# Attention prologue, conversions, projection tile and row-sum constant of a fused attention and feed-forward kernel

## The chip, the cores and the metric

The kernel runs on one core of a Trainium2 chip. The core has TensorE (PE) for matmuls, VectorE (DVE), ScalarE (ACT), GpSimd (POOL) and SyncE (SP), which here only issues DMAs; each engine works through its own queue in order, and semaphores order the queues against each other. The metric is the device time in microseconds, median of several runs; smaller is better. [...]

## The reference

Three stages follow each other. Attention works on 2 batches x 8 heads of 768 tokens with 64 columns. Six random projections give each query and key a bucket of six sign bits, and a query sees only keys of its bucket:

```python
q_bits = (np.einsum('bhsd,dk->bhsk', q, proj) > 0)      # likewise k_bits
mask = q_bucket[:, :, :, None] == k_bucket[:, :, None, :]
scores = np.where(mask, scale * q @ k.T, -1e9)
attn = np.exp(scores - scores.max(-1))
attn = attn / (attn.sum(-1) + 1e-09);  out = attn @ v
```

Then comes a feed-forward with a rational activation, on 1536 tokens: `h = x @ w_in` (512 to 2048), `g = P(h) / (Q(h) + 1e-6)`, `g @ w_out`. Last is a mixture of eight experts with ReLU, whose weights per token come from eight rounds of row and column scaling of a softmax. `w_in` and `w_out` arrive as 64-bit floats; everything else is 32-bit.

## The kernel before, in words

Matmul operands are split into a rounded upper half and a remainder, the lower half (`split`, L95), so that a product is three fast matmuls instead of a slow one.

**Heads.** `load_head` (L119) loads q, k and v of a head into one of two buffers. `prep_head_a` (L225) splits them (head 0's q and k on VectorE, all else on GpSimd), transposes q and k on TensorE against the identity `idr`, and lets ScalarE copy the result into `a1` and `b1`, of which two DMAs make the lower rows of `a2` and `b2`. `prep_head_b` (L251) multiplies by the projections in two column pieces, 512 and 256, each in a single bank (`hp`); VectorE compares each piece with thresholds `thr` into `bits`, and two DMAs put these rows into `a2` and `b2`. Scores multiply `a1` by `b1` and `a2` by `b2` into the same sum, so that unequal buckets push a score down.

**Groups.** A head has three groups of two query tiles, 48 groups in all, one for each iteration of the loop at L720. `scores` (L270) makes four matmuls for each of the two tiles into one of two double banks (`s`); VectorE copies the tile and accumulates its minimum (the scores are negated), and ScalarE takes the exponential with the row sum as its accumulator. `norm` (L288) has VectorE add 1e-9 by a reduce over pairs (sum, 1e-9), take the reciprocal, and GpSimd scale the two tiles. Two iterations later `trans` (L298) transposes the scaled tiles on TensorE in three pieces, each through one of four single banks (`pt`), to an upper half (ScalarE, `pth`) and a lower half (VectorE, `ptl`). One iteration after that `values` (L314) multiplies by v. Head preparations stand in the first two iterations of the head before.

**Weights.** A 64-bit tile of 128 columns is loaded raw (`load_weights`, two buffers per matrix) and converted (`prep_weights`, L188): ScalarE's absolute value and GpSimd's clamp (`narrow_a`), four integer and float operations on VectorE (`narrow_b`, L173), GpSimd's addition (`narrow_c`), ScalarE's upper half, GpSimd's lower half. Eight conversions (four tiles of each matrix) are written into attention at iterations 35, 38, 41 and 44 (`wprep`, L718); there their scratch `c` lies in SBUF. Those of later quarters run in the feed-forward, with scratch in PSUM.

**Order.** In the prologue and in attention the order on each engine is not the written one: a planner sorts the instructions by its own model of their times and may pull one far forward. So the first two conversions (L180 to L183) run before the first scores, and the constants of the feed-forward (L722 to L738) stand in VectorE's queue in the middle of the prologue. From the feed-forward on (L806) the written order is kept on TensorE, ScalarE, VectorE and GpSimd. Its first part has 48 steps; each makes a hidden tile (`gemm1`, one of three banks `h`), its activation (`activate_a`, L366: ScalarE, GpSimd's product `tq`, VectorE's five operations), and from step 6 on also the second product (`gemm2_a`).

## Time and profile before

| | us |
|---|---|
| runs: median (lowest to highest) | 1589.35 (1587.63 to 1591.01) |
| profiled execution, its time | 1589.4 |
| its span | 1587.6 |
| TensorE busy | 1536.8 (97%) |
| VectorE busy | 1199.3 (76%) |
| GpSimd busy | 938.9 (59%) |
| ScalarE busy | 622.1 (39%) |
| in attention, mean of one: minimum (768 columns, VectorE) | 0.949 |
| lower half of transposed weights (512 columns, VectorE) | 0.682 |
| scaling (768 columns, GpSimd) | 0.937 |
| split of q (384 columns, GpSimd): upper half, lower half | 0.531, 1.013 |

Busy time is the time in which an engine had an instruction in work; for TensorE this includes matmuls whose neighbours wait. A share over the whole span mixes three stages with different limits: attention (to about 291 us), the first feed-forward (to about 640 us) and the experts, where TensorE is busy without a gap. What the first two stages wait for is read from their own stretches.

### The profile page before, as it was taken

The numbers are of one execution on the slowest core, as the hardware profiler recorded it, in microseconds if no ns is written. First come the engines' busy times: TensorE is split into PE (matmuls) and PEld (weight loads), VectorE is DVE, ScalarE is ACT, GpSimd is POOL, SyncE is SP. The second block draws the span as 40 slices with busy tenths as digits, with TensorE's granted clock in tenths as the row PEclk, the third lists the DMA queues.
The fourth block names the chain that finished last, engine by engine and source line by source line (L and its number), as shares of the span: only waits on it lengthen the run. The fifth ranks groups of instructions, "written<-read, shape, count | busy, mean of one in ns | idle before, by whom it ended". The sixth has DMA issues, their size and how long they took to land.

```text
span 1587.6 us, 22241 instructions
## 1 busy us (share of the span) xinstructions
PE 1536.8 (97%) x8071; PEld 1355.8 (85%) x8071; DVE 1199.3 (76%) x2116; ACT 622.1 (39%) x1167; POOL 938.9 (59%) x1165
## 2 busy tenths in 40 slices
PE   5989999899999999999999999999999999999999
PEld 4888889687777877889899999989899998989898
DVE  7989999799999984886666766676666666666665
ACT  4878888788777842111111111111111111111111
POOL 6777875577777976456644653564465356436530
PEclk8999999999999999999999999999999999999999
DMA  5322221021212000101010110101011001101002
GB/s 170 86 83 79 81 70 25 14 67 54 66 53 67 14 27 27 41 27 40 27 41 27 41 40 27 36 32 40 27 40 41 27 28 40 40 27 40 14 1 80
DMA packets 49406, 71.85 MB, mean 45 GB/s; under 512 B 4368, under 2 KB 35088, under 8 KB 49296
## 3 DMA queue, kind: packets, MB, share of 16 engines
q1 hardware_dynamic: 48432, 68.85, 14.1%
q8 instruction: 64, 1.05, 0.3%
q10 hardware_dynamic: 864, 1.57, 0.3%
q14 instruction: 46, 0.38, 0.1%
HBM read 59.79 MB, written 3.15 MB: 40 GB/s over the span
## 4 chain that ended last, share of the span: by engine, by line
PE 65%; DVE 2%; ACT 0%; issue 0%; DVEq 0%; ACTq 0%
PE accb L599 33%; PE prod L534 29%; PE acca L405 2%; PE h L354 1%; PE lp L635 0%; DVE t L470 0%; DVE t L473 0%; DVE c L559 0%; DVE part L417 0%; DVE gl L555 0%; ACT xb L106 0%; DVE t L480 0%; ACT gh L554 0%; DVE t L484 0%; DVE csum L676 0%
## 5 line engine op out<-in xcount | busy, mean ns | idle before, releaser
L534 PE MATMUL prod<-xb,ww 128*128 128x384 f32 x2688 | 481.7, 336 | 1.8 <-ACT m L106 1.3
L599 PE MATMUL accb<-wb,gh 128*128 128x512 f32 x1536 | 475.7, 391 | 2.9 <-ACT osum L106 2.5
L534 PEld LDWEIGHTS prod<-xb,ww 128*128 128x128 f32 x2688 | 469.8, 188 | 8.0 <-ACT m L106 1.6
L610 DVE SCALAR_TENSOR_TENSOR osum<-accb,gp,osum 128x512 f32<-128x512 f32 x336 | 251.7, 749 | 127.7 <-PE accb L599 126.0
L599 PEld LDWEIGHTS accb<-wb,gh 128*128 128x128 f32 x1536 | 287.0, 188 | 60.9 <-ACT osum L106 2.9
L599 PE MATMUL accb<-wb,gl 128*128 128x512 f32 x768 | 300.9, 392 | 0.4 <-DVE gl L555 0.4
L100 POOL TENSOR_SCALAR wb<-rb 128x512 fp32r<-128x512 f32 x64 | 40.2, 627 | 405.8 <-PE accb L599 405.8
L554 ACT ACTIVATE gh<-c 128x384 fp32r<-128x384 f32 x256 | 134.3, 526 | 352.5 <-DVE c L559 352.1
L106 ACT ACTIVATE m<-prod 128x384 f32<-128x384 f32 x64 | 31.5, 492 | 457.9 <-PE prod L534 457.9
L599 PEld LDWEIGHTS accb<-wb,gl 128*128 128x128 f32 x768 | 144.2, 188 | 32.0 <-DVE gl L555 1.7
L555 DVE SCALAR_TENSOR_TENSOR gl<-c,gh 128x384 fp32r<-128x384 f32 x256 | 165.2, 645 | 1.3 <-ACT gh L554 0.9
L559 DVE TENSOR_TENSOR c<-prod,u 128x384 f32<-128x384 f32 x192 | 106.6, 558 | 61.7 <-PE prod L534 54.1
L354 PE MATMUL h<-xh,wa 128*128 128x512 f32 x384 | 126.7, 392 | 3.4 <-DVE tu L377 3.4
L405 PE MATMUL acca<-gh,wb 128*128 128x512 f32 x384 | 126.4, 391 | 2.8 <-DVE part L417 1.7
L109 DVE TENSOR_TENSOR ptl<-pt,pth 128x512 fp32r<-128x512 f32 x144 | 94.5, 682 | 19.1 <-ACT pth L106 18.3
L559 DVE TENSOR_TENSOR c<-prod,m 128x384 f32<-128x384 f32 x64 | 35.7, 558 | 92.4 <-PE prod L534 92.4
L103 POOL TENSOR_TENSOR ww<-ra,ww 128x256 fp32r<-128x256 f32 x128 | 95.4, 746 | 10.7
L294 POOL TENSOR_SCALAR e<-e,rs 128x768 f32<-128x768 f32 x96 | 88.8, 937 | 20.8 <-DVE rs L292 11.3
L308 PE MATMUL pt<-idr,e 128*128 128x128 f32 x576 | 83.0, 279 | 11.1 <-DVE ptl L109 4.9
L285 DVE TENSOR_SCALAR_CACHE_REDUCE e<-s 128x768 f32<-128x768 f32 x96 | 90.9, 949 | 2.1 <-PE s L278 1.7
L286 ACT ACTIVATE e<-e,nm 128x768 f32<-128x768 f32 x96 | 89.9, 936 | 3.8 <-DVE e L285 3.1
L354 PEld LDWEIGHTS h<-xh,wa 128*128 128x128 f32 x384 | 72.1, 188 | 22.4 <-DVE tu L377 5.9
(168 smaller groups left out, 2546.3 us busy)
## 6 DMA issues: line engine op xcount, KB each, us to landing
ra<-in_moe_w_dram SPq DMA_DIRECT2D x32, 512.0 KB
rb<-in_moe_w_dram SPq DMA_DIRECT2D x32, 512.0 KB
ra<-in_moe_w_in_dram SPq DMA_DIRECT2D x16, 512.0 KB
rb<-in_moe_w_out_dram SPq DMA_DIRECT2D x16, 512.0 KB
qkv<-in_q_dram SPq DMA_DIRECT2D x16, 192.0 KB
qkv<-in_k_dram SPq DMA_DIRECT2D x16, 192.0 KB
qkv<-in_v_dram SPq DMA_DIRECT2D x16, 192.0 KB
a<-a SPq DMA_DIRECT2D x16, 192.0 KB
```

Source lines behind the costliest of these rows:

```text
L103: pool.tensor_tensor(lo, src, hi.bitcast(F32), ALU.subtract)
L109: dve.tensor_tensor(lo, src, hi.bitcast(F32), ALU.subtract)
L285: dve.tensor_scalar(e[j], s[:, 0:S], BIG, None, ALU.min, ALU.min, accum_out=nm)
L286: act.activation(e[j], e[j], AF.Exp, bias=nm, scale=-1.0, accum_out=rs[:, j, 0:1])
L354: pe.matmul(hps, lhsT=a[:, c], rhs=x[:, c], start=m == 0, stop=m == 3 * KC - 1)
L405: pe.matmul(o, lhsT=l[:, js], rhs=r, start=f == 0 and m == 0, stop=f == QF - 1 and m == 2)
L534: pe.matmul(o, lhsT=w[:, i, c], rhs=x[:, j, c], start=n == 0, stop=n == 5)
L554: act.activation(gh, c, AF.Relu)
L555: low.append(lambda: dve.scalar_tensor_tensor(gl, c, 0.0, gh.bitcast(F32), ALU.max, ALU.subtract))
L559: dve.tensor_tensor(c, o, x, ALU.add)
L599: pe.matmul(o, lhsT=l[:, ts], rhs=r, start=n == 0 and m == 0, stop=n == 1 and m == 2)
L610: dve.scalar_tensor_tensor(d, o, gate["p"][:, n, e:e + 1], d, ALU.mult, ALU.add)
```

## The change

- **Prologue.** proj is loaded between k and v of head 0. The identity is rounded by ScalarE instead of VectorE. The thresholds are made ahead of head 0's preparation. Head 0's compared bits are sent by SyncE and ScalarE, one DMA each. Head 2's load, the raw weights' loads and the constants' loads are ordered behind these sends; the constants move from iteration 2 to 10.
- **Projections.** The two column pieces go into one double bank, taken from the two that the scores use, and are compared by one instruction of 768 columns.
- **Row sums.** The row sums have a tile of their own, and GpSimd adds 1e-9; the reciprocal stays on VectorE.
- **Conversions.** In attention run six of the eight, cut into pieces: two chains of three, a piece of each at set iterations from 4 to 41, ordered behind that iteration's minimum on VectorE, exponential on ScalarE and scaling on GpSimd. Their VectorE scratch lies in PSUM (a single bank). Two conversions, of `w_out`'s tiles 2 and 3, move to the start of the feed-forward.

`tc.issue_after(x)` orders what its block makes behind instruction x in the queue of x's engine; it adds no semaphore.

```diff
-    def narrow_b(bits, c):
-        ci = c.bitcast(I32)
-        pc = sum_bank(3, "bits") if bits_in_psum else c
-        pi = pc.bitcast(I32)
+    def narrow_b1(bits, c, pi):
+        dve.tensor_scalar(pi, c.bitcast(I32), 5, 2, ALU.logical_shift_left, ALU.logical_shift_right)
+        high = bits[:, :, 1]
+        dve.scalar_tensor_tensor(high, high, -0x40000000, pi, ALU.bitwise_and, ALU.bitwise_or)
+
+    def narrow_b2(bits, pi):
...
-            narrow_b(bits, n)
+            if in_attention:
+                narrow_b1(bits, n, bank("bits").bitcast(I32))
+                yield
+                narrow_b2(bits, bank("bits").bitcast(I32))
+            else:
+                pi = sum_bank(3, "bits").bitcast(I32)
+                narrow_b1(bits, n, pi)
+                narrow_b2(bits, pi)
...
+        hp = two_banks("hp").rearrange("p a n -> p (a n)")
         for n0, n1 in COLS:
-            hp = bank("hp")[0:KROW + 2 * NB, 0:n1 - n0]
...
-            dve.tensor_scalar(bits[QROW:KROW + 2 * NB, n0:n1], hp[QROW:], ...)
+        compared = dve.tensor_scalar(bits[rows], hp[rows, 0:S], thr[rows, 0:1], thr[rows, 1:2], ALU.is_ge, ALU.mult)
+        sent = sp.dma_start(a2[QROW:QROW + 2 * NB].bitcast(F32), ...)
+        sent_k = (sp if i else act).dma_start(b2[QROW:QROW + 2 * NB].bitcast(F32), ...)
...
-        dve.tensor_reduce(rs, rs_eps, AX.X, ALU.add)
+        pool.tensor_scalar(rs, rsum, 1e-9, None, ALU.add)
         dve.reciprocal(rs, rs)
...
-    wprep = {NG - 13 + 3 * j: j for j in range(QF)}
+    converting = [convert((0, 0), (0, 1), (0, 3)), convert((1, 0), (1, 1), (0, 2))]
+    CSTEPS = 3 * 5 + 1
+    csteps = {}
+    for m in range(2):
+        for n in range(CSTEPS):
+            csteps.setdefault(4 + m + n * (NG - 9) // CSTEPS, []).append(m)
...
+        for m in csteps.get(it, ()):
+            with behind(minimum, exped, scaled):
+                next(converting[m], None)
...
-    narrowing, acting, summing = [], [], []
+    narrowing, acting, summing = [prep_weights(1, i) for i in (2, 3)], [], []
...
+        for w in narrowing + narrowing:
+            go(w)
         for s in range(NS + QF):
```

## Rows read from the trace of the kernel before

**Rows 1.** The page, part 1: busy us, share of span, instructions.

```profile
PE 1536.8 (97%) x8071; PEld 1355.8 (85%) x8071; DVE 1199.3 (76%) x2116; ACT 622.1 (39%) x1167; POOL 938.9 (59%) x1165
```

**Rows 2.** Stretches: length, busy PE, PEld, DVE, ACT, POOL, clock, DMA share, GB/s.

```profile
0.00:24.20 24.20, 9.49 (x48) 7.13 (x48) 17.31 (x48) 6.43 (x12) 16.03 (x25) 0.95 0.62 178
24.20:291.10 266.90, 252.08 (x1813) 228.00 (x1814) 241.09 (x533) 215.27 (x453) 196.19 (x241) 0.97 0.26 72
```

**Rows 3.** Timeline, prologue: start, duration, engine, line, instruction [idle before and releaser].

```profile
4.54 0.56 DVE L109 TENSOR_TENSOR sk<-qkv,sk 128x384 fp32r<-128x384 f32 x1
...
6.42 0.43 DVE L699 CAST pjr<-pjz 128x512 fp32r<-128x512 f32 x1
...
9.40 0.21 DVE L135 CAST idr<-eye 128x128 fp32r<-128x128 f32 x1
...
9.67 1.00 PE L245 MATMUL tp<-idr,sq 128*128 128x128 f32 x6 [9.67 <-DVE rowf L705]
...
13.61 1.21 DVE L180 TENSOR_SCALAR c<-c 128x512 int32<-128x512 int32 x1 [2.29 <-POOL c L170]
...
13.86 0.63 PE L259 MATMUL hp<-b,pjr 128*108 128x256 f32 x2
...
18.13 0.76 SPq L263 DMA_DIRECT2D b<-bits  x1
...
20.53 0.47 PE L278 MATMUL s<-b,a 76*128 76x512 f32 x1 [1.42 <-DMA b<-bits]
...
24.20 0.96 DVE L285 TENSOR_SCALAR_CACHE_REDUCE e<-s 128x768 f32<-128x768 f32 x1
```

**Rows 4.** Stretch of attention, instructions on tile c alone: DVE, ACT, POOL busy.

```profile
24.20:291.10 266.90, 22.17 (x24) 8.47 (x13) 20.13 (x21) 0.97 0.26 72
```

**Rows 5.** Line 180 by forms: duration ns least/median/most, first and last start.

```profile
L180 DVE TENSOR_SCALAR bits<-c x24: 685/689/690, 308.9 to 507.8; 128x512 int32<-128x512 int32 x24
L180 DVE TENSOR_SCALAR c<-c x8: 405/893/1220, 13.6 to 177.7; 128x512 int32<-128x512 int32 x8
```

**Rows 6.** VectorE, 24.2 to 291.1: waits (total, times, longest), then groups.

```profile
DVE ptl L109 <- ACT pth L106: 18.3, 17, 2.4
...
L260 DVE TENSOR_SCALAR bits<-hp,thr 44x512 fp32r<-44x512 f32 x14 | 11.5, 820 | 0.5
L260 DVE TENSOR_SCALAR bits<-hp,thr 44x256 fp32r<-44x256 f32 x15 | 8.3, 556 | 0.1
```

**Rows 7.** Timeline, VectorE: a reduce of row sums and what follows.

```profile
269.32 0.15 DVE L291 TENSOR_REDUCE rs<-rse 128x2 f32<-128x4 f32 x1
269.41 0.96 DVE L285 TENSOR_SCALAR_CACHE_REDUCE e<-s 128x768 f32<-128x768 f32 x1
```

**Rows 8.** Timeline, TensorE without waits: projections, then values, scores, transposes.

```profile
257.94 0.63 PE L259 MATMUL hp<-a,pjr 128*108 128x512 f32 x2
...
259.33 0.40 PE L277 MATMUL s<-b,a 128*128 128x512 f32 x1
...
264.04 0.96 PE L323 MATMUL av<-pth,sv 128*128 128x256 f32 x6
...
265.56 0.40 PE L277 MATMUL s<-b,a 128*128 128x512 f32 x1
...
266.27 1.04 PE L308 MATMUL pt<-idr,e 128*128 128x128 f32 x8
267.06 0.48 PE L277 MATMUL s<-b,a 128*128 128x512 f32 x1
```

**Rows 9.** GpSimd, 24.2 to 291.1: a wait, and a group.

```profile
POOL e L294 <- DVE rs L292: 11.3, 11, 2.5
...
L100 POOL TENSOR_SCALAR xh<-xp 128x256 fp32r<-128x256 f32 x23 | 9.5, 413 | 12.1 <-DVE xp L334 12.1
```

**Rows 10.** Timeline, start of the feed-forward.

```profile
294.52 1.29 POOL L375 TENSOR_TENSOR tq<-tq,tw 128x512 f32<-128x512 f32 x1 [2.15 <-ACT tq L373]
...
295.14 0.69 DVE L376 TENSOR_TENSOR tu<-tu,h 128x512 f32<-128x512 f32 x1 [4.08 <-ACT tu L374]
...
304.93 0.50 PE L354 MATMUL h<-xh,wa 128*128 128x512 f32 x1 [1.06 <-DVE tu L377]
...
311.96 1.04 POOL L186 TENSOR_TENSOR c<-ra 128x512 f32<-128x512 f32 x1 [1.95 <-DVE ra L183]
```

More of the change, by code (lines that the diff above doesn't have):

```diff
@@ L6 @@
-from contextlib import ExitStack
+from contextlib import ExitStack, contextmanager, nullcontext
 from itertools import count
@@ L72 @@
     FP = F2 // P // 2
-    WLOAD = 3
-    CONST_AT = 2
+    WLOAD = 2
+    CONST_AT = 10
     EB = 6
@@ L117, with load_head @@
     loaded = {}
-    def load_head(i):
+    def load_head(i, between=None):
         b, h = heads[i]
@@ L122, in load_head, with load_proj @@
         for j, src in enumerate((q, k, v)):
+            if j == 2 and between:
+                between()
             sp.dma_start(t[:, j], src[b, h].rearrange("(p c) d -> p c d", c=C))
         loaded[i] = t
-    load_head(0)
     pj = ap.tile([P, NB], F32, tag="pj", bufs=1, name="pj")
-    sp.dma_start(pj[0:D, :], proj)
-    sp.dma_start(pj[D:2 * D, :], proj)
+    def load_proj():
+        sp.dma_start(pj[0:D, :], proj)
+        sp.dma_start(pj[D:2 * D, :], proj)
+    load_head(0, load_proj)
     load_head(1)
@@ L233, in prep_head_a @@
             hi, lo = (dve.tensor_copy, dve_lo) if i == 0 and j < 2 else (pool_hi, pool_lo)
-            split(hi, lo, d[:, :, h0:h0 + D], d[:, :, l0:l0 + D], t[:, j])
-        if i + 2 < len(heads):
+            with tc.issue_after(last) if i == 1 and j == 2 else nullcontext():
+                made = split(hi, lo, d[:, :, h0:h0 + D], d[:, :, l0:l0 + D], t[:, j])
+            if j == 1:
+                splitted, last = made, made.ins
+        if 0 < i < len(heads) - 2:
             load_head(i + 2)
@@ L683, with behind @@
     NG = len(heads) * G
-    prep_head_a(0)
-    pjz = ap.tile([P, 4, P], F32, tag="e", bufs=EB, name="pjz")
-    dve.memset(pjz, 0.0)
-    pjh = ap.tile([P, NB], F32R, tag="pjh", bufs=1, name="pjh")
-    dve.tensor_copy(pjh, pj)
-    pjl = ap.tile([P, NB], F32, tag="pjl", bufs=1, name="pjl")
-    dve.tensor_tensor(pjl, pj, pjh.bitcast(F32), ALU.subtract)
-    for j, row, half in ((0, QROW, slice(0, P)), (1, QROW, slice(0, D)), (2, KROW, slice(0, P)), (3, KROW, slice(D, P))):
-        src = pjh.bitcast(F32) if j % 2 == 0 else pjl
-        dve.tensor_scalar(pjz[half, j, row:row + NB], src[half], -1.0, None, ALU.mult)
-        dve.tensor_copy(pjz[half, j, row + NB:row + 2 * NB], src[half])
-    pjr = ap.tile([P, 4, P], F32R, tag="pjr", bufs=1, name="pjr")
-    dve.tensor_copy(pjr, pjz)
+    @contextmanager
+    def behind(*made):
+        with ExitStack() as stack:
+            for m in made:
+                stack.enter_context(tc.issue_after(m.ins))
+            yield
     row = ap.tile([P, 1], I32, tag="row", bufs=1, name="row")
@@ L713 @@
     dve.tensor_scalar(rowf[:, 2:3], rowf[:, 0:1], -1.0, F_BELOW, ALU.add, ALU.mult)
-    dve.tensor_tensor(thr[:, 0:1], thr[:, 0:1], rowf[:, 2:3], ALU.add)
-    prep_head_b(0)
-    wprep = {NG - 13 + 3 * j: j for j in range(QF)}
-    bits_in_psum = False
+    thr_made = dve.tensor_tensor(thr[:, 0:1], thr[:, 0:1], rowf[:, 2:3], ALU.add)
+    with behind(thr_made):
+        first_split, _ = prep_head_a(0)
+    pjz = ap.tile([P, 4, P], F32, tag="e", bufs=EB, name="pjz")
+    dve.memset(pjz, 0.0)
+    pjh = ap.tile([P, NB], F32R, tag="pjh", bufs=1, name="pjh")
@@ new lines @@
+    with behind(first_split):
+        dve.tensor_copy(pjh, pj)
+    pjl = ap.tile([P, NB], F32, tag="pjl", bufs=1, name="pjl")
+    dve.tensor_tensor(pjl, pj, pjh.bitcast(F32), ALU.subtract)
+    for j, row, half in ((0, QROW, slice(0, P)), (1, QROW, slice(0, D)), (2, KROW, slice(0, P)), (3, KROW, slice(D, P))):
+        src = pjh.bitcast(F32) if j % 2 == 0 else pjl
+        dve.tensor_scalar(pjz[half, j, row:row + NB], src[half], -1.0, None, ALU.mult)
+        dve.tensor_copy(pjz[half, j, row + NB:row + 2 * NB], src[half])
@@ new lines, with convert @@
+    pjr = ap.tile([P, 4, P], F32R, tag="pjr", bufs=1, name="pjr")
+    dve.tensor_copy(pjr, pjz)
+    sent, sent_k, compared = prep_head_b(0)
+    with behind(sent):
+        load_head(2)
+    in_attention = True
+    def convert(*which):
+        for m, i in which:
+            yield from prep_weights(m, i)
+    converting = [convert((0, 0), (0, 1), (0, 3)), convert((1, 0), (1, 1), (0, 2))]
[4 more added lines that the diff above has]
+            csteps.setdefault(4 + m + n * (NG - 9) // CSTEPS, []).append(m)
@@ L738 @@
             dve.memset(dbias, 1.0 + 1e-6)
+            late_on_dve.close()
         if it == WLOAD:
-            for c in range(2):
-                load_weights(0, c)
-                load_weights(1, c)
+            with behind(sent):
+                for m, c in ((0, 0), (1, 0), (0, 1), (1, 1)):
+                    load_weights(m, c)
         i, g = divmod(it, G)
@@ L745 @@
         if it < NG:
-            scores(it, 0)
+            scored, minimum, exped = scores(it, 0)
         if i + 1 < len(heads) and g < 2:
-            (prep_head_a, prep_head_b)[g](i + 1)
+            with behind(*((sent_k,), (scored, minimum), ())[min(it, 2)]):
+                (prep_head_a, prep_head_b)[g](i + 1)
         if 0 <= ti < NG:
@@ L753 @@
         if it < NG:
-            scores(it, 1)
+            _, minimum, exped = scores(it, 1)
         if 0 <= ti < NG:
@@ L758 @@
         if it < NG:
-            norm(it)
-        if it in wprep:
-            for m in range(2):
-                list(prep_weights(m, wprep[it]))
+            scaled = norm(it)
+        for m in csteps.get(it, ()):
+            with behind(minimum, exped, scaled):
+                next(converting[m], None)
+    for w in converting:
+        list(w)
     qkv_pool_stack.close()
```

56 lines of the change are left out of this document (29 added, 27 removed).

## The prediction

> **What bounds the kernel now.** The page comes first. TensorE is busy for 97% of the span [rows 1], so only some 51 us can come from its idle time; but matmuls are pipelined, and a busy TensorE that waits for a drained buffer still reads as busy. So the second view is the table by stage. The change touches the prologue, the attention and the start of the first feed-forward; from about 330 us on every instruction stays. In the table the attention runs from the first minimum of the scores (24.20 us) to its last value sum (291.1 us). In these 266.9 us VectorE is busy 241.1 us (90%), GpSimd 196.2 us (74%) [rows 2]. Third, the timeline up to 24.20 us says why attention starts so late [rows 3]: the identity for the transposes stands on VectorE behind work that waits for constants and is cast only at 9.40, the transposes start at 9.67, and after the last projection matmul (13.86) VectorE is inside a weight conversion (from 13.61). The score matmul waits for the compared bits' DMA until 20.53, and the first minimum waits on VectorE behind the second conversion until 24.20. Fourth, VectorE's groups and waits inside attention [rows 6]: of its 25.8 idle us (266.9 - 241.1), 18.3 are the lower half of the transposed weights waiting for ScalarE's upper half, 17 times, 2.4 us at most. That is TensorE's transposes coming late, not ScalarE being slow. So attention is bound by VectorE, with TensorE close behind, as the next part shows.
>
> **The change part by part.** The profiled execution took 1589.4 us: its span of 1587.6 and 1.8 around it. That is the median of the runs shown (1589.35), so no correction is needed.
>
> *Prologue.* The identity goes to ScalarE, the thresholds are made while q is still loading, proj is loaded ahead of v, the constants move to iteration 10, and no conversion runs here. The last split of head 0's k ended at 5.10 (4.54 + 0.56), which is when all transposes can go. From the transposes' start to the end of the last projection matmul it took 14.49 - 9.67 = 4.8 us before; proj's tiles (ready at 6.85) are no later than the transposes' copies. So projections end at 9.9. One wide compare (1.08, worked out below) gives 11.0. The key rows' DMA, issued at 18.13, released its matmul at 20.53, 2.4 us later; the two sends now leave from two queues at once: 13.4. What is left of the first score tile takes about 1.2 us: the first minimum starts near 14.6 instead of 24.20. **Term 1: -9.6 us** (bounds: -6 if the queue of loads behind proj delays k; -11.5 if the projections run without the gaps they had).
>
> *Conversions.* Six conversions had all or nearly all of their VectorE work inside attention, 22.2 us for 24 instructions [rows 4], 0.92 each. They wrote their scratch into SBUF. In the feed-forward the same instruction writes to PSUM and takes 0.689 at any of 24 times; with SBUF scratch it took 0.405 to 1.220, median 0.893 [rows 5]. The change gives attention's conversions PSUM scratch: 6 x 4 x 0.689 = 16.5, so -5.7 (bounds: 0 if PSUM gains nothing beside a busy GpSimd, -8 with the faster ends). Pieces are ordered behind the iteration's minimum, exponential and scaling on all three engines, so a GpSimd piece no longer stands ahead of a scaling; I put no term on this but count it among the waits below.
>
> [...]
>
> *Row sums.* 48 reduces leave VectorE. Their rows last 0.15, but the next instruction starts 0.09 after [rows 7], so -4.3 (bounds: -2.9 to -7.2). In their place GpSimd gets 48 adds of 128x2. No such row exists: its 128x256 scaling takes 0.413 [rows 9], an upper bound; the lower is nothing. I take 0.2, half of it, since fixed cost dominates: 9.6 us on GpSimd, less 3.6 for conversion work that leaves it. It would be 202 us busy in about 249, 81%, so the add itself is hidden as long as VectorE does not stand waiting for it. What is queued behind that wait is VectorE's reciprocal and all its later minima; this is a rival below.
>
> *Wide projection tile.* Two compares of 512 and 256 columns take 0.820 and 0.556 [rows 6]; 256 columns cost 0.264, so 768 take 1.084, 0.29 less a head. One of head 1's stood before 24.20, so inside attention the sum falls by 3.6 us (19.8 - 15 x 1.084). The matmuls are the same eight. But the wide tile takes one of the two double banks that the scores use, and frees two of the four single ones.
>
> *Attention together.* VectorE: 241.1 - 5.7 - 4.3 - 3.6 + 1.5 (the constants' small operations, moved in) = 229.0. If all its idle time stayed: 254.8. TensorE's floor, from starts in a stretch where it does not wait [rows 8]: values 1.52, two score tiles 2 x 0.71, twelve transposes 12 x 0.79 / 8 = 1.19, together 4.13 a group; a head's preparation 1.39 for projections and another 1.19 for its transposes. 48 x 4.13 + 15 x 2.58 = 236.9. So TensorE becomes the bound, and only the waits between 236.9 and 254.8 are open. I take 249, somewhat above the middle, because nothing shortens the chain scaling, transpose, upper half, lower half. **Term 2: -18 us** (bounds -12 and -29).
>
> *Start of the feed-forward.* Two conversions move here. After the last value sum VectorE idled 4.08 us up to its first polynomial operation at 295.14 [rows 10]. Two conversions (2 x 2.76) can begin near 293.0, after two clamps that follow the last split, and end at 298.5; GpSimd's additions (1.04 each, the last at 299.5) stand ahead of the first product, which started at 294.52. That product is 5.0 us later, and ScalarE's logarithm and the following steps with it. TensorE hides part at first with three free banks, but already waited 1.06 us for that chain at 304.93. **Term 3: +5 us** (bounds 0, if the scheduler finds earlier gaps, and +7).
>
> Sum: -9.6 - 18 + 5 = -22.6; 1589.4 - 22.6 = 1567 us. The case's own range: -36 to -10, that is 1553 to 1579.
>
> **The rivals.** *Wide tile against score buffers.* Each head's projections hold one of two score buffers for 1.39 us plus the wait for VectorE's compare. If VectorE reaches the compare one lower half and one minimum late (0.68 + 0.95 by the small table), TensorE has one score buffer for that long, and loses about 1 us for each of 15 heads: 1567 + 15 = 1582. For it: VectorE is nearly full. Against: a seventh tile on six costs a full VectorE nothing, and it waited for scores only rarely.
>
> *Attention doesn't move.* If VectorE's freed time all turns into waiting for transposes that are late for GpSimd's sake, term 2 shrinks to some -2, and the rest is -9.6 + 5: 1583; with the prologue at its worse bound 1587, no change. For it: 18.3 us of such waits already [rows 6]; against: many follow from conversion pieces on GpSimd, which are reordered.
>
> *The handshake of the row sums, the slower side.* VectorE's reciprocal now waits for GpSimd's add. An add that finds GpSimd inside a pair of scalings or a split (1.9 and 1.5 us by the small table) makes VectorE stand still in the middle of its queue. The price is the mean stall times 48; it decides from 22.6 / 48 = 0.47 us. At 0.7 us, less than half a pair, it costs 33.6 and the time is 1601. For it: GpSimd already waited 11.3 us for reciprocals, 11 times [rows 9], so both sides meet closely. Against: with the queue ordered well the add directly follows the exponential and finds GpSimd idle.
>
> **How the numbers follow.** Forecast 0.62, wide tile 0.15, attention doesn't move 0.14 (of it 0.05 within 0.2%), handshake 0.09. A measurement tells no less than about 0.2%, 3.2 us, from no change. Faster: 0.62 + 0.15 + 0.09 = 0.86; same 0.05; slower 0.09. The range reaches from 1552 to 1586: it takes in the first two cases and most of the third, and leaves out the handshake and a few hundredths below.
>
> **What would show it.** Term 1: the first minimum near 14.6 us and no conversion before it. Term 2: VectorE near 229 us busy between the first minimum and the last value sum, that stretch near 249 us, conversion operations at 0.69. Term 3: the first polynomial operation about 7.4 us after the last value sum instead of 4.1. The handshake would show as VectorE's idle time before reciprocals, the wide tile as TensorE waiting for the compare or for minima. The prediction is wrong if the attention stretch stays above 260 us, or if the gain of attention comes back as idle TensorE in the feed-forward.

## The result: slower, and outside the range

The changed kernel took 1609.05 us (median of 4 runs, 1608.03 to 1609.68), the kernel before, in the runs taken with it, 1589.55; the ratio is 1.0121 [1.0105, 1.0137]. Forecast were 1567 us and a range of 1552 to 1586. The rival on the slower side, the handshake of the row sums at 1601 us, is what happened.

The profiled execution has a span of 1606.8 us against 1587.6. The marks that the prediction named divide the 19.2 us:

| | before | forecast | after |
|---|---|---|---|
| first minimum starts, us | 24.20 | 14.6 | 16.51 |
| attention, first minimum to last value sum, us | 266.9 | 249 | 290.6 |
| from there to the end, us | 1296.5 | +5 | 1299.7 |

So -7.7 + 23.7 + 3.2 = 19.2. Two of the three terms came out with the sign and nearly the size that was given to them; attention grew where it was to shrink.

First the page's part 1 of the changed kernel, which answers to [rows 1]: VectorE has 11.5 us less work in 69 instructions fewer, GpSimd 48 instructions more, and TensorE is busy 8.1 us more for the same 8071 matmuls (at the same mean granted clock, 0.994 of the full one), while its share of the span falls.

```profile
PE 1544.9 (96%) x8071; PEld 1359.3 (85%) x8071; DVE 1187.8 (74%) x2047; ACT 625.0 (39%) x1168; POOL 942.3 (59%) x1213
```

Then the stretches of the changed kernel, in the columns of [rows 2] (the clock is the one granted to TensorE, as a share of the full one):

```profile
0.00:16.50 16.50, 8.28 (x38) 6.88 (x39) 6.98 (x26) 4.87 (x10) 7.30 (x16) 1.00 0.48 133
16.50:307.10 290.60, 259.70 (x1824) 230.85 (x1824) 234.55 (x478) 218.48 (x454) 203.26 (x293) 0.98 0.25 70
```

VectorE's busy time in attention fell, from 241.1 to 234.5 us, but its idle time rose from 25.8 to 56.0. The sum of the two is the whole story: -6.6 + 30.2 = 23.6. VectorE's waits in that stretch (instruction, what it waits for, total us, times, longest) say where the idle time is:

```profile
DVE rs L308 <- POOL rs L307: 31.7, 38, 3.5
DVE ptl L109 <- ACT pth L106: 15.4, 16, 1.9
```

The first line didn't exist before: 38 of the 48 reciprocals wait for GpSimd's add, 31.7 us in all, 0.66 us a group. The second is the wait of [rows 6], 18.3 then. GpSimd's own longest wait in the stretch shows the other side of the handshake:

```profile
POOL rs L307 <- ACT e L301: 42.0, 20, 5.0
```

In 20 groups GpSimd came to its add too early and stood 42.0 us for the exponential, in front of all that is queued behind; in the others it came late. The add itself is as small as was estimated (0.2, half of the 0.413 that 128x256 take in [rows 9]): duration least/median/most in ns, first and last start.

```profile
L307 POOL TENSOR_SCALAR rs<-rsum x48: 212/213/218, 20.7 to 299.5; 128x2 f32<-128x2 f32 x48
```

One late group in the timeline, rows picked out (start, duration, engine, line, instruction; in brackets the idle time before it and what ended it):

```profile
237.43 0.19 ACT L301 ACTIVATION_READ_ACCUMULATOR e<-e,nm 128x1 f32 x1
237.50 0.54 POOL L100 TENSOR_SCALAR sk<-qkv 128x384 fp32r<-128x384 f32 x1
238.13 1.01 POOL L103 TENSOR_TENSOR sk<-qkv,sk 128x384 fp32r<-128x384 f32 x1
239.11 0.41 POOL L100 TENSOR_SCALAR xh<-xp 128x256 fp32r<-128x256 f32 x1
239.60 0.74 POOL L103 TENSOR_TENSOR xl<-xp,xh 128x256 fp32r<-128x256 f32 x1
240.43 0.21 POOL L307 TENSOR_SCALAR rs<-rsum 128x2 f32<-128x2 f32 x1
240.68 0.17 DVE L308 RECIPROCAL rs<-rs 128x2 f32<-128x2 f32 x1 [3.52 <-POOL rs L307]
```

The sums are there at 237.62 (237.43 + 0.19). GpSimd then runs two splits, of the next head's keys and of a value sum, 2.8 us that have nothing to do with the sums, and only then an add of 0.21. VectorE stands for 3.52 us, and behind its reciprocal stand the next minima: ScalarE then idles 3.10 us up to its next exponential (241.84) and TensorE 1.99 us (up to 242.40). Gone through group by group in this way (the end of the second sum's read against the end of the GpSimd instruction ahead of the add), 19 of the 38 waits, 25.8 of the 31.7 us, had GpSimd in other work for over 0.1 us after the sums were ready. The other 19 waits, 5.9 us, were the bare trip over a second engine, 0.20 to 0.53 us each.

### The profile page after: what moved, and what is told of

The parts are those of the page before. It is cut to its first block, busy times and chain, and to the rows that moved or that the text cites. A ratio compares the mean times of both kernels' runs of the same rounds, so it can differ in the third digit from the quotient of the medians.

```text
span 1606.8 us, 22235 instructions
## 1 busy us (share of the span) xinstructions
PE 1544.9 (96%) x8071; PEld 1359.3 (85%) x8071; DVE 1187.8 (74%) x2047; ACT 625.0 (39%) x1168; POOL 942.3 (59%) x1213
## 4 chain that ended last, share of the span: by engine, by line
PE 64%; DVE 2%; ACT 0%; issue 0%; DVEq 0%; ACTq 0%
PE accb L616 32%; PE prod L551 28%; PE acca L422 2%; PE h L371 1%; PE lp L652 0%; DVE t L487 0%; DVE t L490 0%; DVE c L576 0%; DVE part L434 0%; DVE gl L572 0%; ACT xb L106 0%; DVE t L497 0%; ACT gh L571 0%; DVE t L501 0%; DVE csum L693 0%
## 5 line engine op out<-in xcount | busy, mean ns | idle before, releaser
L109 DVE TENSOR_TENSOR ptl<-pt,pth 128x512 fp32r<-128x512 f32 x144 | 94.7, 684 | 16.3 <-ACT pth L106 15.4
```

Source lines behind the costliest of these rows:

```text
L109: return dve.tensor_tensor(lo, src, hi.bitcast(F32), ALU.subtract)
```

## The experiments

Theories: **handshake** (VectorE stands for GpSimd's add; within it, the place in GpSimd's queue or the bare trip), against **wide tile** (the projections take a score buffer), **ordered pieces** (conversions behind minimum, exponential and scaling come at bad times), and **given back** (what the prologue saves moves into attention). Runs of one group shared a chip and the runs of the kernel before; between groups, a difference by the two ratios to the kernel before is the fairer one and is given where it differs. "Without the 1e-9" means that the constant is left out of the row sums, which each hold a 1 from the minimum's own exponential.

### The handshake, undone and alone

Row sums back on VectorE, with the tiles of pairs (sum, 1e-9), all else as changed:

```diff
-        pool.tensor_scalar(rs, rsum, 1e-9, None, ALU.add)
+        dve.tensor_reduce(rs, rsum, AX.X, ALU.add)
```

> The changed kernel with one part undone: VectorE adds 1e-9 again by its reduce over pairs, all else as changed. Handshake theory: VectorE's 31.7 us of waiting for GpSimd's add go, 48 reduces cost some 4 to 7 us, so 1609 - 31.7 + 5 = about 1582 us, VectorE idle in attention near 26 us instead of 56. Wide-tile theory (the projections hold a score buffer): the waits only move to another instruction, 1600 to 1609. Ordered-pieces theory (conversion pieces in the three queues make the stalls): also 1600 or more.

No add at all:

```diff
-        pool.tensor_scalar(rs, rsum, 1e-9, None, ALU.add)
-        dve.reciprocal(rs, rs)
+        dve.reciprocal(rs, rsum)
```

> The changed kernel without the addition of 1e-9 to the row sums (left out; every row sum holds exp(0) = 1, so the fp32 sum is the same with it). VectorE's reciprocal reads ScalarE's sums directly. Handshake theory: 1609 - 31.7 = about 1577 us, and 4 to 7 us below the run with VectorE's reduce. Wide-tile and ordered-pieces theories: 1600 or more.

Only the projection tile back in two narrow pieces:

```diff
-        hp = two_banks("hp").rearrange("p a n -> p (a n)")
...
         for n0, n1 in COLS:
+            hp = bank("hp")[0:KROW + 2 * NB, 0:n1 - n0]
...
+            compared = dve.tensor_scalar(bits[rows, n0:n1], hp[QROW:], thr[rows, 0:1], thr[rows, 1:2], ALU.is_ge, ALU.mult)
```

> The changed kernel with the projections back in two single banks and two compares; GpSimd still adds 1e-9. Wide-tile theory: the score buffers are free again, 1590 to 1597. Handshake theory: within 5 us of 1609, since two compares cost VectorE 0.2 to 0.3 us more a head (16 heads, 3 to 5 us) and the waits for the add stay near 31 us.

And the GpSimd add alone, in the kernel before, with the row sums in a tile of their own:

```diff
-        dve.tensor_reduce(rs, rs_eps, AX.X, ALU.add)
+        pool.tensor_scalar(rs, rs_eps, 1e-9, None, ALU.add)
```

> The kernel before with one part done alone: GpSimd adds 1e-9 instead of VectorE's reduce. Handshake theory: VectorE waits for the add some 0.4 to 0.7 us a group, 20 to 33 us, less 4 to 7 for the reduces: 1602 to 1618. The other theories: no loss, 1583 to 1591.

Measured, against 1589.49 before: sums on VectorE 1588.28 (ratio 0.9994 [0.9985, 1.0003]); no add 1583.54 (0.9964 [0.9951, 0.9977]); narrow tile 1607.61 (1.0115 [1.0098, 1.0132]); the add alone 1611.3 (1.0141 [1.0124, 1.0157]). Undoing one instruction a group takes away 20.8 us (1609.05 - 1588.28; 20.2 by ratios), adding it alone to the old kernel costs 21.8 (1611.3 - 1589.49). The edit has the same price in either surrounding, and the wide tile is out: taking it back moves 1.4 us (1.0 by ratios), inside the intervals.

One more cause has to be kept apart: the planner sorts anew when an instruction changes its engine. Against the changed kernel, up to the last value sum, 490 of VectorE's 502 instructions and 248 of GpSimd's 256 stand in the same order in the kernel without an add (the add itself left out of the count), but only 466 and 223 in that with the sums on VectorE. So the 25.5 us between the changed kernel and that without an add (25.0 by ratios) are hardly a new order's; the 20.8 us can hold some of it.

The stretch and VectorE's waits in the kernel before with the add alone:

```profile
23.87:311.20 287.33, 255.51 (x1813) 226.64 (x1814) 236.92 (x485) 217.28 (x453) 207.15 (x289) 0.98 0.24 67
```

```profile
DVE rs L289 <- POOL rs L288: 33.8, 33, 2.7
DVE ptl L109 <- ACT pth L106: 5.8, 8, 1.1
```

The same wait appears there, without any other part of the change; of its 33.8 us, 30.0 came from GpSimd being in other work. The second line is a reading that is easily missed: the waits for the upper half of the transposed weights fell from 18.3 to 5.8 us, for a VectorE that stands for one thing arrives later at the next. So VectorE's idle time in attention rose by 24.6 us (25.8 to 50.4) and not by the 33.8 of the new wait, and its work fell by 4.2.

The expectations of about 1582 for the sums on VectorE and about 1577 for no add were missed by 6 and 6.5 us, though the verdict between the theories stands. The stretch of the kernel with the sums on VectorE and VectorE's waits are the base on which the rest is measured:

```profile
15.60:286.70 271.10, 251.83 (x1819) 228.52 (x1818) 236.22 (x526) 216.57 (x454) 192.71 (x246) 0.97 0.28 75
```

```profile
DVE ptl L109 <- ACT pth L106: 14.9, 13, 1.8
DVE rs L310 <- ACT e L304: 7.0, 12, 1.1
```

Even without the handshake attention takes 271.1 us, 4 more than before, at 4.9 us less VectorE work: idle time is 34.8. That had to be explained too.

### Where the add waits, and what else holds attention up

The reciprocal (with the scalings) issued behind the next group's first minimum:

```diff
         rs = ap.tile([P, 2], F32, tag="rs", bufs=4, name="rs")
         pool.tensor_scalar(rs, rsum, 1e-9, None, ALU.add)
+        return e, rs
+
+    def norm_2(e, rs):
         dve.reciprocal(rs, rs)
...
             scored, minimum, exped = scores(it, 0)
+            if it:
+                with behind(minimum):
+                    scaled = norm_2(*summed_rows)
```

> The changed kernel, GpSimd's add kept, but VectorE's reciprocal and GpSimd's two scalings are issued one step later: the reciprocal behind the first minimum of the next group in VectorE's queue. Theory queue place (the loss is that the reciprocal stands too early in VectorE's queue, so VectorE waits for a sum that is not there yet): most of the 31.7 us of waiting before reciprocals goes, under 8 us stay, and the time is 1580 to 1592. Theory engine change (any trip from ScalarE through GpSimd to VectorE costs this much, or the later scaling delays the transposes as much): still 1600 or more.

Sums on VectorE and the narrow tile together (both edits as above):

> The changed kernel with VectorE's reduce for the row sums (measured 1588.3) and with the projections back in two single banks: only prologue, pieces and the two moved conversions are left of the change. Wide-tile theory (the double bank taken from the scores costs what VectorE saves): 1580 or less. Ordered-pieces theory (pieces at fixed places in three queues cost it): 1586 to 1593, two compares more or less.

Sums on VectorE, and all eight conversions in attention, none in the feed-forward:

```diff
-    converting = [convert((0, 0), (0, 1), (0, 3)), convert((1, 0), (1, 1), (0, 2))]
-    CSTEPS = 3 * 5 + 1
+    converting = [convert(*((m, i) for i in range(QF))) for m in range(2)]
+    CSTEPS = 4 * 5 + 1
...
-    narrowing, acting, summing = [prep_weights(1, i) for i in (2, 3)], [], []
+    narrowing, acting, summing = [], [], []
```

> The changed kernel with VectorE's reduce (1588.3) and with all eight conversions in pieces in attention, none at the start of the feed-forward. If the feed-forward's start costs what the traces show (last value sum to the end 3.2 us longer than before) and a conversion costs attention its 2.76 us of VectorE: 1588.3 - 3.2 + 5.5 = 1590.6, so no gain, 1587 to 1594. Ordered-pieces theory: pieces cost more than their own time, 1592 to 1600.

Sums on VectorE, and the six conversions issued whole, two at a time and in no order behind the group's work:

```diff
+    wprep = {NG - 13: ((0, 0), (1, 0)), NG - 10: ((0, 1), (1, 1)), NG - 7: ((0, 2), (0, 3))}
...
-        for m in csteps.get(it, ()):
-            with behind(minimum, exped, scaled):
-                next(converting[m], None)
+        for m, n in wprep.get(it, ()):
+            list(prep_weights(m, n))
```

> The changed kernel with VectorE's reduce (1588.3) and its six conversions in attention no longer in ordered pieces: each written whole at iterations 35, 38 and 41 and placed by the planner alone, as in the kernel before (scratch in PSUM stays). Ordered-pieces theory: attention's idle VectorE time falls from 34.9 us back to about 26, 1579 or less. Wide-tile theory: no change, 1586 to 1591.

Measured, against 1588.59 before: later reciprocal 1592.94 (1.0027 [1.0017, 1.0037]); narrow tile too 1589.79 (1.001 [1.0001, 1.0019]); eight 1594.03 (1.0035 [1.0022, 1.0048]); unordered 1594.79 (1.0039 [1.0024, 1.0054]).

VectorE's waits with the later reciprocal:

```profile
DVE rs L311 <- POOL rs L307: 22.3, 18, 2.7
```

One minimum between the add and the reciprocal brought 16.1 us back (1609.05 - 1592.94; 14.9 by ratios), three quarters of what the kernel with the sums on VectorE has over the changed one. The time lies 0.9 us above the range of the theory of the queue place and 7 us below that of the engine change. Of the 19 short trips 3 are left: of the 18 waits, 15 with 20.2 us had GpSimd in other work. The expectation of under 8 us of waits was wrong, so the waits that remain hang on where the add lands in GpSimd's queue. The time returned is more than the 9.4 us of waits that went; a VectorE that has done its minimum before it stands leaves work to TensorE and ScalarE, but that reason is argued, not shown.

With the sums on VectorE the narrow tile is 1.5 us slower (1589.79 against 1588.28; 2.5 by ratios), with the add on GpSimd it was 1.4 faster; the wide tile takes 2.8 us of work off VectorE (236.22 against 239.05) and moves the time by nothing that these intervals tell apart. The unordered pieces are 6.5 us worse than the ordered ones (7.2 by ratios), outside what either theory expected, so the order was no loss; TensorE's granted clock in attention was 0.94 in that run against 0.97. With all eight conversions in attention the rest, from the last value sum on, took 1296.4 us, against 1299.8 with two of them behind attention. That is Term 3 by itself, 3.4 us; but attention took 279.0 instead of 271.1, 4.0 us for each of the two conversions and not the 2.76 of their VectorE work, so the time is the one that the theory of ordered pieces gave (1592 to 1600).

A further cause of idle time showed in ScalarE's waits of the kernel with the sums on VectorE:

```profile
ACT c L174 <- POOL wa L103: 3.7, 3, 1.2
ACT c L174 <- POOL wb L103: 2.7, 2, 1.6
```

They add up to 6.4 us, against 1.9 us of such waits before. (Before, ScalarE also stood 15.4 us, 7 times, for GpSimd's additions ahead of the upper halves `wa` and `wb`; those waits are gone, so in all ScalarE waits less for conversions than it did.) A chain takes its pieces one after another, and the first piece of its next conversion, on ScalarE, came in the same step as GpSimd's last piece of the one before, whose scratch buffer it needs. Such a place in the timeline of the same kernel, rows picked out:

```profile
107.99 1.28 POOL L103 TENSOR_TENSOR wa<-c,wa 128x512 fp32r<-128x512 f32 x1
109.30 0.67 ACT L174 ACTIVATE c<-ra 128x512 f32<-128x512 f32 x1 [1.21 <-POOL wa L103]
109.88 0.92 ACT L304 ACTIVATE e<-e,nm 128x768 f32<-128x768 f32 x1
110.80 0.85 ACT L261 ACTIVATE a<-tp 128x512 fp32r<-128x512 f32 x2
111.51 0.63 PE L328 MATMUL pt<-idr,e 128*128 128x128 f32 x4 [1.77 <-ACT a L261]
...
113.84 0.69 DVE L109 TENSOR_TENSOR ptl<-pt,pth 128x512 fp32r<-128x512 f32 x1 [1.77 <-ACT pth L106]
```

And the stretches around it:

```profile
110.00:112.00 2.00, 0.49 (x5) 0.52 (x6) 1.08 (x4) 2.00 (x5) 1.74 (x4) 1.00 0.32 91
112.00:114.00 2.00, 2.00 (x14) 2.00 (x12) 0.23 (x2) 1.81 (x5) 1.92 (x3) 0.60 0.77 244
114.00:116.00 2.00, 2.00 (x11) 2.00 (x11) 1.66 (x4) 1.30 (x3) 2.00 (x4) 0.54 0.60 157
```

ScalarE stands 1.21 us; the exponential and the next head's copies come late by as much, TensorE has only 0.49 us of work in the two us from 110, and its granted clock then falls to means of 0.60 and 0.54 over four us: an estimate from these two means, some 3.4 us at the 0.50 to which it falls in the traces of before (118 to 120 us) and after (243 to 246 us). VectorE's wait for the upper half at 113.84 is the end of that chain. A wait of an engine that has slack (ScalarE is busy 216.6 of 271.1 us) became one of VectorE.

### The buffer wait taken away, and attention without conversions

One empty step between two conversions of a chain, with the sums on VectorE. Either ScalarE's waits for the scratch buffer hold attention up (theory buffer wait: 1578 to 1583 us, those waits under 1 us, VectorE idle for 26 us of attention or less), or such stalls only stand where another would (1586 to 1590):

```diff
             yield from prep_weights(m, i)
+            yield
...
-    CSTEPS = 3 * 5 + 1
+    CSTEPS = 3 * 6
```

> The changed kernel with VectorE's reduce (1588.3), and one empty step between two conversions of a chain, so that ScalarE's first operation of the next conversion is no longer issued in the step of GpSimd's last of the one before, whose scratch buffer it needs. [...]

The same edit, without the 1e-9:

> The same empty step in the kernel without the addition of 1e-9 (left out, 1583.5): buffer-wait theory 1573 to 1579, otherwise 1582 to 1586.

Sums on VectorE, and no conversion in attention (all eight stand one after another ahead of the feed-forward's first step):

```diff
-    converting = [convert((0, 0), (0, 1), (0, 3)), convert((1, 0), (1, 1), (0, 2))]
+    converting = [iter(()), iter(())]
...
-        for w in narrowing + narrowing:
-            go(w)
+        for i in range(QF):
+            for m in range(2):
+                for _ in prep_weights(m, i):
+                    pass
```

> The changed kernel with VectorE's reduce and all eight conversions at the start of the feed-forward, one after the other, none in attention. It splits the price of conversions: attention from first minimum to last value sum should fall from 271.1 us by the six conversions' 16.6 us of VectorE and the waits they cause, to 246 to 254, if conversions are what holds it; if the planner's order of heads and groups holds it, to no less than 258. The feed-forward's start is later by some 8 x 4 to 5 us, so the total is 1595 to 1615.

The empty step, without the 1e-9, and the last two conversions as pieces between the feed-forward's steps instead of ahead of them:

```diff
-        for w in narrowing + narrowing:
-            go(w)
...
+    prep_at(0, 1, 2)
+    prep_at(1, 1, 3)
     for qf in range(NQ - 1):
```

> As the kernel without the addition and with the empty step, and the two conversions of the feed-forward are not ahead of step 0 but pieces of steps 0 to 3, as later conversions are. If it is GpSimd's additions ahead of the first product that make the feed-forward's start late (5.6 us from the last value sum to the first polynomial operation against 4.1, and 3.2 us to the end), 2 to 3 us of it come back: 1571 to 1577. If the conversion's VectorE time itself is the price, no change to the run without this edit.

Measured, against 1588.48 before: empty step 1582.58 (0.9965 [0.9952, 0.9977]); without the 1e-9 too 1578.27 (0.9938 [0.9925, 0.9952]); no conversions in attention 1612.9 (1.0156 [1.014, 1.017]); pieces in the feed-forward 1582.27 (0.9963 [0.9951, 0.9976]).

The stretch of attention with the empty step, of the kernel with the sums on VectorE:

```profile
14.70:280.90 266.20, 252.07 (x1825) 227.97 (x1824) 236.65 (x526) 216.56 (x454) 192.65 (x246) 0.98 0.28 77
```

One wait of 1.2 us (`c` for `wa`) is left of the 6.4, attention shrank by 4.9 us (271.06 to 266.14) and the time by 5.7 (4.6 by the two ratios, which were taken on different chips); 0.9 of it lies ahead of attention. The time came out as the theory of the buffer wait had it; its other two marks, waits under 1 us and idle time of 26 or less, were missed (1.2 and 29.5). TensorE's granted clock over attention was 0.98 against 0.97. The step also moves all later pieces, and the planner then orders other instructions anew (26 of 502 on VectorE), so that the buffer alone is worth these 5 us is likely, not shown. This kernel leaves nothing out and is faster than the kernel before and than the one with the sums on VectorE. Leaving out the 1e-9 as well gives the fastest kernel here; its attention, and below it that of the kernel without conversions in attention:

```profile
16.40:276.90 260.50, 247.70 (x1821) 224.41 (x1819) 233.72 (x478) 216.75 (x454) 191.90 (x245) 1.00 0.28 78
```

```profile
14.70:264.20 249.50, 244.94 (x1820) 224.73 (x1818) 219.65 (x502) 208.91 (x441) 174.85 (x227) 0.99 0.26 69
```

Without conversions VectorE has 16.6 us less to do (236.2 to 219.6), 2.77 for each, which is four times the 0.689 of [rows 5], and attention falls by 21.7 us to 249.4. That fits a VectorE that still paces attention: its time comes back whole, and some idle time with it. But the same edit takes 17.9 us off GpSimd and 7.7 off ScalarE, and which engine's share came back is not told apart. The 249 us of the forecast were reached only with the conversions gone, and behind attention the eight cost 49.8 us (1346.3 for the rest against 1296.5). The pieces between the feed-forward's steps missed both expectations: the first polynomial operation came after 4.06 us as before, but the rest was 1303.8 us instead of 1299.7, so the conversions cost as much between the steps as ahead of them, and more.

### The add on another engine, and its neighbours behind it

ScalarE adds the 1e-9, straight behind its exponentials (eps is a constant tile of 128x1):

```diff
-        pool.tensor_scalar(rs, rsum, 1e-9, None, ALU.add)
+        act.activation(rs, rsum, AF.Identity, bias=eps)
```

> The changed kernel with the 1e-9 added by ScalarE (128x2, right behind the exponential in its queue) instead of GpSimd. Theory foreign queue (25.8 of the 31.7 us of waiting were spent while GpSimd was in other work although the sums were ready): the waits before reciprocals fall under 10 us and the time is 1584 to 1592, near the run with VectorE's reduce (1588.3). Theory any trip (one more engine in the chain costs 20 us): 1600 or more.

The add stays on GpSimd, and the next head's splits are issued behind it:

```diff
-        if i + 1 < len(heads) and g < 2:
+        if i + 1 < len(heads) and g < 2 and not (it > 1 and g == 0):
...
-            scaled = norm(it)
+            added, scaled = norm(it)
+            if it > 1 and g == 0 and i + 1 < len(heads):
+                with behind(added):
+                    prep_head_a(i + 1)
```

> The changed kernel with GpSimd's add kept and a head's preparation issued behind the add of its iteration, so that its six splits on GpSimd stand behind that add instead of ahead of it. Theory foreign queue: waits before reciprocals with GpSimd in splits go in a third of the groups; total waits 10 to 20 us instead of 31.7, time 1592 to 1602 unless the later preparation delays the next head. Theory any trip: waits and time as before, 1605 to 1612.

Measured, against 1589.0 before: 1602.76 (1.0091 [1.0075, 1.0106]) and 1685.06 (1.0609 [1.0592, 1.0627]). On ScalarE the add takes longer (0.294 us at the median, against 0.213), and the wait is small:

```profile
DVE rs L310 <- ACT rs L309: 6.0, 4, 1.8
```

So here a trip over another engine cost little, as that engine is the one that makes the sums: attention took 273.7 us, 16.9 less than with GpSimd, 2.6 more than with the sums on VectorE. The time, 1602.76, missed its expectation all the same and by itself speaks for the other theory (1600 or more); the stretches show that the difference lies in another place. The experts' stage, whose instructions are the same, in this kernel and in that with the sums on VectorE:

```profile
652.00:1600.50 948.50, 943.28 (x4688) 844.26 (x4686) 635.51 (x1072) 155.70 (x300) 467.49 (x649) 1.00 0.10 34
```

```profile
649.40:1586.50 937.10, 931.98 (x4683) 842.83 (x4681) 635.49 (x1072) 155.00 (x299) 465.26 (x649) 1.00 0.10 34
```

TensorE is busy 11.3 us more for the same matmuls at a granted clock of 1.00 in both. From 750 to 1550 us it is busy all the time in both, and gets through 3991 matmuls against 4037, 0.200 us each against 0.198 (an estimate from the counts of its records). Why is open.

With the splits behind the add the waits before the reciprocal fell from 31.7 to 17.9 us, but VectorE now waits for the next head's projections:

```profile
DVE bits L278 <- PE hp L276: 61.7, 15, 7.8
DVE rs L308 <- POOL rs L307: 17.9, 31, 1.6
```

The edit moved the whole preparation behind the add, transposes too, and TensorE stood 82.6 us (14 waits) in those transposes for GpSimd's splits, so its time says nothing of the add. That a better place in GpSimd's queue would remove the handshake is argued from the 25.8 us of foreign work, not shown.

## Why the prediction was wrong, step by step

**The failed step** is in the paragraph on the row sums: "so the add itself is hidden as long as VectorE does not stand waiting for it", with -4.3 us for the reduces. The add itself was foreseen well (0.213 us for 0.2, and GpSimd busy 203.3 / 290.6 = 70% where 81% was forecast), but the condition isn't met: VectorE stood 31.7 us. The term was -4.3 and measured +20.8. The rival that described this was right in its mechanism and in the size of the wait: 0.66 us a group where it took 0.7 and a limit of 0.47. That its time, 1601, lies so near to 1609 is luck in part: the add cost 25.5 us against the kernel without one, and not 33.6, and the other 16 or so of the 42 us over the forecast are mostly the second failure below. Its chance of 0.09 was too small. Two things in the rows spoke for more. A queue that is busy three quarters of the time [rows 2] with instructions of 0.4 to 1.0 us will often be at work when the sums get ready: in 28 of the 48 groups it was. And the reason given against it, that the add "finds GpSimd idle", held in fewer than half of the groups: in 20 it waited for the sums (42.0 us), in the others it came late.

**A reading of [rows 6]** was wrong too, and the same mechanism lay in it. The 18.3 us of waits for the upper half were put down to "TensorE's transposes coming late, not ScalarE being slow". In 14 of the 17 waits, 16.3 us, the transposes had long ended (0.4 to 3.0 us earlier) when ScalarE took them up; it came straight from other work in its queue: exponentials (6.7 us of the waits), a conversion's absolute value (7.3) or a head's copy (2.3). One such place in the kernel before, rows picked out:

```profile
110.39 0.63 PE L308 MATMUL pt<-idr,e 128*128 128x128 f32 x4 [0.43 <-POOL e L294]
113.44 0.69 ACT L169 ACTIVATE c<-ra 128x512 f32<-128x512 f32 x1 [0.48 <-POOL wa L103]
114.03 0.57 ACT L106 ACTIVATE pth<-pt 128x512 fp32r<-128x512 f32 x1
114.63 0.69 DVE L109 TENSOR_TENSOR ptl<-pt,pth 128x512 fp32r<-128x512 f32 x1 [2.40 <-ACT pth L106]
```

The transposes ended at 111.02; ScalarE had stood 2.50 us for GpSimd's addition of a conversion (up to 111.41), had then done a conversion's upper half, an exponential and the next conversion's absolute value, and reached the copy at 114.03. Work that waits for another engine, in a queue that others need: read so, the row was a warning of the handshake.

**Term 1**, -9.6, measured -7.7, within its bounds. The identity is cast by ScalarE at 2.02 and transposes start at 4.72, as forecast. Then proj's tiles, ready at 7.93 (7.23 + 0.70) instead of 6.85, and the send of the compared rows came later:

```profile
6.17 1.00 POOL L103 TENSOR_TENSOR sv<-qkv,sv 128x384 fp32r<-128x384 f32 x1
6.21 0.99 DVE L739 COPY pjz<-pjl 64x6 f32<-64x6 f32 x1
7.23 0.70 DVE L741 CAST pjr<-pjz 128x512 fp32r<-128x512 f32 x1
10.31 0.63 PE L276 MATMUL hp<-b,pjr 128*108 128x256 f32 x2
10.98 1.09 DVE L278 TENSOR_SCALAR bits<-hp,thr 44x768 fp32r<-44x768 f32 x1 [3.05 <-PE hp L276]
12.10 1.59 ACTq L280 DMA_DIRECT2D b<-bits  x1
15.28 0.76 PE L293 MATMUL s<-b,a 76*128 76x512 f32 x1 [1.88 <-DMA b<-bits]
```

These are rows of the prologue's timeline after, which answers to [rows 3]. Proj's tiles came after the transposes' copies (the last ended at 7.12), and TensorE waited 1.62 us for them; what held them is a copy of 64x6 that took 0.99 us where others of its kind take 0.15, and ended with the GpSimd split beside it (7.20 against 7.17). So projections end at 10.94, not 9.9; the compare takes 1.09 as worked out (1.084); from its end to the matmul that needs the rows it is 3.2 us, not 2.4: the issue on ScalarE's queue lasted 1.59 us, that on SP's 0.76 before. Part of the gain is lent: before, GpSimd had done 16.0 us of work when attention began, now 7.3, and nearly all of head 2's splits and head 1's compare lie inside attention. No run undid the prologue alone, so the theory "given back" stays untested.

**Term 2**, -18, fails a second time, apart from the handshake. With the sums back on VectorE the forecast would have been 249 + 4.3 = 253.3; measured were 271.1. VectorE's busy time was foreseen well: 229.0 against 233.5 in the kernel without an add. The groups of the changed kernel account for the difference:

```profile
L278 DVE TENSOR_SCALAR bits<-hp,thr 44x768 fp32r<-44x768 f32 x15 | 16.3, 1086 | 0.8 <-PE hp L276 0.3
L181 DVE TENSOR_SCALAR bits<-c 128x512 int32<-128x512 int32 x7 | 4.7, 675 | 0.0
L775 DVE TENSOR_SCALAR ab<-cb 128x2 f32<-128x2 f32 x1 | 1.0, 1036 | 0.0
L771 DVE CAST wg<-wg 128x32 fp32r<-128x32 f32 x1 | 1.0, 1027 | 0.0
```

The conversions take 0.68 an instruction as forecast, a gain of 5.9 for 5.7, and the wide compare 1.086. (Six conversions are 24 instructions, 16.3 us in the kernel without an add; the seventh of the second row is the feed-forward's.) The constants' small operations came to 2.6, not 1.5, two of them 1.0 each; the reduces gave back 2.7 here (236.2 to 233.5), not 4.3, and the wide compare 2.8, not 3.6. That is 1.1 + 1.6 + 0.8 = 3.5 of the 4.5. What failed is the choice "I take 249, somewhat above the middle": idle time was to fall from 25.8 to 20, and in every changed kernel that kept conversions in attention it was 26.7 or more. TensorE's floor of 236.9 was never reached; the nearest is the 249.4 without conversions. The bound with all idle time kept, 254.8, was near: the best kernel has 260.4, with 4.7 us more busy time and 0.9 more idle. Of the 9 us by which idle time rose without the handshake, 5 went with the empty step (34.8 to 29.5), most likely the buffer wait on ScalarE, which the prediction didn't see because it costed the pieces by engine and not by the buffer that they hand on. The cause of the other 4 is open.

**The first rivals.** The wide tile against score buffers is refuted: 1.0 us one way and 2.5 the other by ratios, where it was priced at 15. "Attention doesn't move", 1583, comes near in its number to the change with the sums on VectorE (1588.3, of which 4.3 are the reduces it keeps) and to that without an add (1583.5), but not in its mechanism: VectorE's waits for upper halves fell, from 18.3 to 14.9 us with the sums on VectorE. What rose there were its waits for sums (1.1 before, 7.0), for scores (1.7, 6.2) and for the copies of value sums (1.4, 6.1).

**On PSUM scratch** the forecast gave the right size (5.7 us, measured 5.9), by an operation that stands for little of it (L180, [rows 5]). With PSUM scratch the one-input operations took 0.675 to 0.685, against means of 0.56 to 0.80 with SBUF before, and the two-input ones 0.67 to 0.68 against 1.01 to 1.27. One of them, L182 on `ra` (0.56 before), lost; by these means the one-input operations still gave some 0.7 us in all, and the two-input ones 5.4. The ten of before that took over 1.2 us all ran wholly beside GpSimd instructions, as did some short ones.

**Term 3**, +5, measured +3.2, and 3.4 when undone. VectorE's timeline after, which answers to [rows 10]:

```profile
306.67 0.42 DVE L351 TENSOR_TENSOR xp<-av,avt 64x256 f32<-64x256 f32 x1 [1.01 <-ACT avt L106]
307.01 0.68 DVE L181 TENSOR_SCALAR bits<-c 128x512 int32<-128x512 int32 x1
...
312.68 0.68 DVE L393 TENSOR_TENSOR tu<-tu,h 128x512 f32<-128x512 f32 x1
```

The first polynomial operation comes 5.59 us after the last value sum (312.68 - 307.09), not 7.4: the conversions start with the end of that sum, at 307.01, and not 1.9 us later behind the clamps, as was forecast.

## What to carry to other kernels

Before a small operation is given to a second engine, write down what stands in that engine's queue at the moment the operand gets ready: the price is the wait for a place in that queue, paid on the engine that waits (31.7 us here, of which some 20 to 25 reached the time), and not the operation's 0.2 us. If the sum must leave VectorE, give it to the engine that produces its operand (6.0 us of waits on ScalarE against 31.7 on GpSimd, and attention 16.9 us shorter, though that kernel's time was 1602.76 for a reason that is open), or put other work between the add and the instruction that needs it: one minimum there was worth 15 to 16 us. Before a wait is put down to the producer's producer, look at when that one ended: in [rows 6] it was the queue in between. When work is cut into pieces, look at which buffer one piece hands to the next, and leave a step between them: the edit that did so was worth some 5 us here.

## What the runs showed of the hardware

- In the kernel with the sums on VectorE a wait of 1.21 us on ScalarE, which had slack, was followed by 1.5 of 2 us in which TensorE had no work, and the granted clock then had means of 0.60 and 0.54 over 4 us. By these means, an estimate, the lower clock took another 1.7 us of TensorE's full-speed time, on top of the 1.5 without work.
- In the changed kernel operations of VectorE on 128x2 and 128x32 took 1.0 us each (the negation of `cb`, L775, and the cast of `wg`, L771), where a reciprocal of 128x2 takes 0.16. Their ends follow GpSimd's: the cast ended at 69.55 and the negation at 70.50, the GpSimd splits beside them at 69.51 and 70.47. In the traces of before and after, seven operations of up to 128x32 took 0.42 to 1.04 us ahead of the last value sum, and each ended 0.02 to 0.04 us after a GpSimd instruction; 52 others ran wholly beside one and took 0.14 to 0.17 us, so why these seven took longer is open.
- The same TensorE work took 11.3 us more (943.3 against 932.0) over the experts' stage in the kernel with the add on ScalarE than in that with the sums on VectorE, at a granted clock of 1.00 in both. That kernel has one constant tile more; whether this matters, no run tests.
